# A fused attention and two-layer FFN kernel: the first pair's steps in a new order, its mask as a ramp on ScalarE

## The chip, the cores and the metric

The kernel runs on one core of one Trainium2 chip. The metric is the device time of one execution, in microseconds.

## The reference

Attention over 2 batches, 8 heads, 768 positions and head size 64, with a window of `n_local` = 96 keys back, `n_global` = 8 keys that all see, and a linear bias by distance; then two feed-forward layers on 1536 tokens of width 512 (inner width 2048), the second with a rational activation.

```
scores = q k^T / sqrt(D)
is_global = pos_k < n_global;   is_local = (0 <= rel) & (rel < n_local),  rel = pos_q - pos_k
dist = n_local where global and not local, else |rel|
scores = where(global or local, scores - slope_h * dist, -1e9)
x = softmax(scores) v                      # heads put side by side: 1536 x 512
x = max(0.01 h, h) w_out,   h = x w_in     # first layer
y = (P(h) / (Q(h) + 1e-6)) w_out,  h = x w_in   # second layer, P cubic, Q quadratic in |h|
```

## The kernel before

**Pairs and units.** Attention is done by pairs of heads, 8 pairs in all (`P_`), in a window: a block of 128 queries sees its own block of keys and a slot with the block before it, whose first 32 columns hold the global keys. A pair has 6 blocks times 2 heads = 12 units (`U`); unit n has block i = (n mod 12) // 2 and head j = n mod 2. Block 0 has 128 columns of scores, the others 256. Each value of q and k is kept as a high and a low fp32r part (`qh`, `ql`, `kh`, `kl`), and a unit's scores are three passes on TensorE (line 440): `qh kh`, `qh kl`, `ql kh`. Units of head 0 and head 1 use different halves of the array and are issued side by side.

**A unit's steps.** `scores` (L440) writes 256 columns of one of two PSUM banks, `sc0` for head 0 and `sc1` for head 1; even blocks take the first half of the bank, odd blocks the second. `least` (L451, VectorE) adds the bias, stores `sn` and reduces to the least value. `exp` (L465, ScalarE) makes `pr`. `transposes` (L476, TensorE) and `evacuate` (L482 on ScalarE or L484 on VectorE) make `pts`. `values` (L495 to 498, TensorE) multiplies by v, and `finish` (L504 to 507) divides.

**A pair's preparation.** k: transposes on TensorE (L324, for pair 0 L383), `kh` on ScalarE (L334, L400), `kl` on VectorE (L336, L402), then the slots are copied (L349 to 352: on GpSimd; for pair 0 those of `kl` on ScalarE). q: transposes, then for pair 0 `qh` on ScalarE (L413) and `ql` on VectorE (L415); for later pairs `qt` on ScalarE (L362) and `qh`, `ql` on GpSimd (L364, L365). These are generators; each `next` issues one step. Pair 0 loads and prepares blocks 0 and 1 first (`q0`, `k0`), then the further blocks 2 to 5 (`q1`, `k1`); later pairs take two halves of three blocks.

**What sets the order.** Everything here is in a hand-written order: each engine executes its own instructions in the order in which the program issues them, and semaphores hold them until their inputs are there. The loop over n (L638 to 661) issues for each n: scores of the units in `GROUPS[n]`, `least` of those in `LEASTS[n]`, `exp` of unit n - 1, transposes and evacuation of unit n - 3, values of unit n - 5, `finish`, and then `fillers(n)`, which advances each running generator by one step and starts new ones: the next pair's preparation at the slots of `PREP0` (pair 0) or `PREP`, the loads of later pairs, and the decoding of float64 weights into fp32 parts from n = 10 on. From unit 8 on, the scores of four units are issued together. `k1` and `q1` start in `fillers(0)`, behind the scores and reductions of units 0 and 1.

**Ahead of the loop** (L519 to 553): loads on SyncE's and ScalarE's DMA queues, twelve TensorE fillers (`keep_busy`, L531, products of ones that nothing reads), the distance table (`window_bias`), first transposes, the two numbers spread over the partitions by a small product (L538), the mask for block 0 (`far`, L244 and L246), the bias (`near`, L250) and its half for head 1 (`half`). The mask of the other part is made behind the first two reductions. SyncE's queue then holds pair 1's k, half of pair 0's v, pair 1's q, and the other half of v.

**After attention** the two layers follow: 96 blocks of products with 512 columns, TensorE without a pause; the first weights are decoded in attention's fillers.

Of the kernel before, what the change touches and what calls it, by code (L numbers as in the profile page):

```python
# [8 lines left out]
F32 = mybir.dt.float32  # L9
# [8 lines left out]
P = 128  # L18
GW = 32
MAX_LOCAL = P - GW + 1  # L20
QK_BOUND = 7000.0
EPS_Q = 1.0 + 1e-6
FAR = 2.56e11


@with_exitstack
def attention_moe_moe2(
# [26 lines left out]
    NTILE = NT // TT  # L54


    PREP0 = (("prep_k", 4, 0), ("prep_q", 5, 0), ("prep_k", 8, 1), ("prep_q", 9, 1))
    PREP = (("prep_k", 0, 0), ("prep_q", 1, 0), ("prep_k", 4, 1), ("prep_q", 6, 1))
    LOAD_K = 4
    LOAD_V = 6  # L60
# [1 line left out]
    XOUT = (8, 9)  # L62

    FIRST = 8
    BUSY = (12, 3, 8)
    XOUT_LAST = (2, 8)
    AHEAD_STEPS = {93: (0,), 94: (0,), 96: (0,), 97: (0,), 98: (1,), 99: (1,)}
    FIRST_ACT = 98
# [22 lines left out]

    ints = cpool.tile([1, 4], I32, name="ints")
    intf = cpool.tile([1, 4], F32, name="intf")
    num1 = cpool.tile([1, 2], F32, name="num1")
    ones = cpool.tile([1, P], F32, name="ones")
    nums = cpool.tile([P, 2], F32, name="nums")
    n_loc = nums[:, 0:1]
    n_glo = nums[:, 1:2]

# [3 lines left out]
    def read_ints():  # L103
        nc.vector.tensor_copy(intf, ints)
        lo, hi = (intf.rearrange("p (j w) -> p j w", w=2)[:, :, w] for w in range(2))
        nc.vector.scalar_tensor_tensor(hi, lo, 0.0, hi, ALU.is_lt, ALU.add)
        nc.vector.scalar_tensor_tensor(num1, hi, 4294967296.0, lo, ALU.mult, ALU.add)

    coef = cpool.tile([P, 8], F32, name="coef")

# [110 lines left out]
    def window_bias(bpool, rpool):  # L221

        misc = rpool.tile([P, 2 * DM], I32, tag="raw", name="misc")
        rel_i = misc[:, 0:BW]
        dist = bpool.tile([P, BW], F32, name="dist")
        mask = bpool.tile([P, BW], F32, name="mask")
        nc.gpsimd.iota(rel_i[:, W2:BW], [[-1, P]], base=0, channel_multiplier=1)
        nc.gpsimd.iota(rel_i[:, 0:W2], [[-1, W2]], base=P, channel_multiplier=1)
        col_i = bpool.tile([P, GW], I32, name="col_i")
        nc.gpsimd.iota(col_i, [[1, GW]], base=0, channel_multiplier=0)  # L230

        nc.vector.tensor_copy(dist, rel_i)
        nc.vector.tensor_scalar(mask, dist, 0.0, 8192.0, ALU.is_lt, ALU.mult)
        nc.vector.tensor_tensor(dist, dist, mask, ALU.add)
        col = bpool.tile([P, GW], F32, name="col")
        nc.vector.tensor_copy(col, col_i)
        bias = bpool.tile([P, 2, BW], F32, name="bias")

        def part(first):
            return slice(W2, BW) if first else slice(0, W2)  # L240

        def far(first):
            cs = part(first)
            nc.vector.tensor_scalar(mask[:, cs], dist[:, cs], n_loc, FAR, ALU.is_ge, ALU.mult)  # L244
            gs = slice(cs.start, cs.start + GW)
            nc.vector.scalar_tensor_tensor(mask[:, gs], col, n_glo, mask[:, gs], ALU.is_ge, ALU.mult)  # L246

        def near(first):
            cs = part(first)
            nc.vector.scalar_tensor_tensor(bias[:, 0, cs], dist[:, cs], n_loc, mask[:, cs], ALU.min, ALU.add)  # L250

        def half(first):
            cs = part(first)
            if first:
                nc.vector.tensor_scalar(bias[:, 1, cs], bias[:, 0, cs], 0.5, None, ALU.mult)
            else:
                nc.scalar.activation(bias[:, 1, cs], bias[:, 0, cs], AF.Copy, scale=0.5)

        return bias, far, near, half

    def attention(wpool, w1, ffn):
        with ExitStack() as actx:
# [26 lines left out]
            class Pair:  # L289
# [77 lines left out]
                def load_first(self, s):  # L367
                    if s == 0:
                        self.first = {
                            n: apool.tile([P, NB, 2, D], F32, tag=f"{n}r", name=f"{n}r", bufs=2)  # L370
                            for n in "qk"
                        }
                    b = slice(*((0, 2), (2, NB))[s])
                    for name, src in (("q", q), ("k", k)) if s == 0 else (("k", k), ("q", q)):
                        for j, queue in enumerate((nc.sync, nc.scalar if s == 0 and name == "k" else nc.sync)):
                            r = src[self.b, 2 * self.hp + j].rearrange("(i p) d -> p i d", p=P)
                            queue.dma_start(self.first[name][:, b, j], r[:, b])

# [154 lines left out]
            keep_busy(BUSY[0])  # L533
            bias, bias_far, bias_near, bias_half = window_bias(bpool, rpool)
            next(q0)
            read_ints()
            spread = ps.tile([P, W2], F32, tag="pt", name="spread")[:, 0:2]
            nc.tensor.matmul(spread, ones, num1, start=True, stop=True)  # L538
            next(k0)
            keep_busy(BUSY[1])  # L540
            next(q0)
            next(k0)
            nc.vector.tensor_copy(nums, spread)
            bias_far(True)
            next(q0, None)
            next(k0)
            next(k0, None)
            bias_near(True)
            bias_half(True)
            P_[1].load_k()  # L550
            P_[0].load_v((0,))
            P_[1].load_q()
            P_[0].load_v((1,))

            early = []
            for f in range(NF_EARLY):
# [26 lines left out]
            def start(g):  # L583
                next(g)
                running.append(g)

            def fillers(n):

                p, s = divmod(n, PU)
                for g in list(running):  # L590
                    if next(g, running) is running:
                        running.remove(g)
                new = []
                if p + 1 < len(P_):
                    nxt = P_[p + 1]
                    for what, slot, half in PREP0 if p == 0 else PREP:
                        if s == slot:
                            new.append(getattr(nxt, what)(half))
                    if s == LOAD_V:
                        nxt.load_v()  # L600
                    if s == LOAD_K and p + 2 < len(P_):
                        P_[p + 2].load_k()
                    if s == LOAD_Q and p + 2 < len(P_):
                        P_[p + 2].load_q()
                if 0 < p < len(P_):
                    for half, slot in enumerate(XOUT if p < len(P_) - 1 else XOUT_LAST):
                        if s == slot:
                            new.append(P_[p - 1].x_out(half))
                if n in DECS and early:
                    new.append(decode(*early.pop(0)))  # L610
                if n == PU:
                    load_coef()
                if n == 2 * PU:
                    prepare_coef()
                if n == FIRST_ACT:
                    ffn.act_1(0, ([], []))
                for u in AHEAD_STEPS.get(n, ()):
                    ffn.h_step(u)
                if n == 0:
                    start(k1)  # L620
                    start(q1)
                if n == 1:
                    bias_half(False)
                for g in new:
                    start(g)

            def unit(n):
                return U[n] if 0 <= n < len(U) else None

            LV = 5  # L630
            GROUPS = {m: (m,) for m in range(0, FIRST, 2)}
            GROUPS.update({m: (m, m + 2) for m in range(FIRST, len(U), 4)})

            LEASTS = {m: (m, m + 1) for m in range(0, FIRST, 2)}
            for m in range(FIRST, len(U), 4):
                LEASTS[m], LEASTS[m + 1] = (m, m + 1), (m + 2, m + 3)
            n = 0
            while n < len(U) or running or n <= len(U) + LV + 1:  # L638

                for m in GROUPS.get(n, ()):  # L640
                    for _ in zip(unit(m).scores(), unit(m + 1).scores()):
                        pass
                    if n == 2:
                        keep_busy(BUSY[2])
                for m in LEASTS.get(n, ()):
                    unit(m).least()
                    if m == 1:
                        bias_far(False)
                        bias_near(False)
                for m in (0, 1) if n == 1 else (n - 1,):  # L650
                    if n != 2 and unit(m):
                        unit(m).exp()
                if unit(n - 3):
                    unit(n - 3).transposes()
                    unit(n - 3).evacuate()
                if unit(n - LV):
                    unit(n - LV).values()
                if unit(n - LV - 1) and unit(n - LV - 1).ih == HB - 1 and unit(n - LV - 1).j == 1:
                    unit(n - LV - 1).finish()
                fillers(n)  # L660
                n += 1
# [484 lines left out]
```

## Time and profile before

| | us |
|---|---|
| time, median of 3 runs (lowest, highest) | 637.1 (636.68, 637.37) |
| the profiled execution's own time | 637.13 |
| its span, first to last instruction | 635.3 |
| TensorE busy in the span | 626.5 |
| VectorE, ScalarE, GpSimd busy | 469.1, 439.1, 206.9 |

The span is the profiler's, the time includes what lies around it. In the rows below engines are PE (TensorE matmul), PEld (its weight load), DVE (VectorE), ACT (ScalarE), POOL (GpSimd), SP (SyncE); a q behind the name means the engine's instruction queue, for example a DMA issue. L440 is line 440 of the kernel. A row with x2 covers two instructions, and its duration runs from the start of the first to the end of the last. Matmuls are pipelined, so rows of PE overlap. In brackets stands the idle time of the engine just before, and what ended it.

### The profile page before, as it was taken

To read this page: it belongs to the slowest core of one execution; us is meant where nothing else is said; L and a number is where in the kernel's file an instruction comes from. 1 tells how busy PE (TensorE), PEld (TensorE's weight loads), DVE (VectorE), ACT (ScalarE), POOL (GpSimd) and SP (SyncE) were. 2 spreads that over 40 slices of the span, in tenths; PEclk is the share of its full clock that TensorE was granted. 3 is DMA by queue.
4 is the path that set the end of the run, shared out by engine and by line. 5 is a ranking of instruction groups with operands and counts; after the bars stand their busy time and mean duration, and the time that the engine had idled before them with its cause. 6 is when DMAs were issued, how large, how long until landed. Compare 5 with 4: busy or idle time off the path is not lost.

```text
span 635.3 us, 9655 instructions
## 1 busy us (share of the span) xinstructions
PE 626.5 (99%) x3289; PEld 527.7 (83%) x3289; DVE 469.1 (74%) x931; ACT 439.1 (69%) x831; POOL 206.9 (33%) x221
## 2 busy tenths in 40 slices
PE   8999999999999999999999999999999999999996
PEld 7999998888888888888888888888888888888884
DVE  6888888878877545456444489998777777897785
ACT  6888988768776545455444377876677888876672
POOL 3978864443443434341000012222222222112220
PEclk9999999999999999999999999999999999999999
DMA  9987742955267776765322301000033331100002
GB/s 185 222 176 174 165 113 71 311 183 182 81 200 224 229 225 202 245 191 194 99 91 90 91 29 34 1 1 1 0 102 97 101 96 48 68 21 1 2 1 72
DMA packets 80895, 73.34 MB, mean 115 GB/s; under 512 B 50948, under 2 KB 67332, under 8 KB 80836
## 3 DMA queue, kind: packets, MB, share of 16 engines
q1 hardware_dynamic: 80048, 71.12, 39.5%
q0 software_dynamic: 224, 0.92, 0.4%
q8 instruction: 28, 0.46, 0.3%
q10 hardware_dynamic: 564, 0.59, 0.3%
q14 instruction: 31, 0.25, 0.1%
HBM read 60.69 MB, written 11.93 MB: 114 GB/s over the span
## 4 chain that ended last, share of the span: by engine, by line
PE 97%; DVE 2%; ACT 0%; issue 0%; DVEq 0%
PE h L691 41%; PE y L815 21%; PE y L813 21%; PE pt L476 3%; PE sc L440 3%; PE o L498 3%; PE o L497 2%; PE h L324 1%; PE h L209 1%; PE idle L531 0%; PE o L495 0%; DVE sn L451 0%; DVE xl L215 0%; DVE ql L415 0%; DVE kl L402 0%
## 5 line engine op out<-in xcount | busy, mean ns | idle before, releaser
L691 PE MATMUL h<-xh,w 128*128 128x512 f32 x768 | 253.4, 390 | 0.0
L691 PEld LDWEIGHTS h<-xh,w 128*128 128x128 f32 x768 | 144.1, 188 | 29.8
L691 PE MATMUL h<-xl,w 128*128 128x512 f32 x384 | 149.4, 389 | 0.0
L746 POOL TENSOR_TENSOR gl<-u,gh 128x512 fp32r<-128x512 f32 x44 | 57.0, 1296 | 264.4 <-PE y L815 125.4
L813 PE MATMUL y<-gh,w 128*128 128x512 f32 x384 | 126.1, 389 | 0.0
L815 PE MATMUL y<-w,gh 128*128 128x512 f32 x384 | 125.6, 389 | 0.0
L164 POOL TENSOR_TENSOR dec<-dec,wraw 128x512 int32<-128x512 int32 x48 | 63.6, 1334 | 82.7 <-DVE wraw L151 76.3
L813 PEld LDWEIGHTS y<-gh,w 128*128 128x128 f32 x384 | 72.1, 188 | 15.1
L815 PEld LDWEIGHTS y<-w,gh 128*128 128x128 f32 x384 | 72.1, 188 | 15.0
L691 PEld LDWEIGHTS h<-xl,w 128*128 128x128 f32 x384 | 72.2, 188 | 14.5
L815 PE MATMUL y<-w,gl 128*128 128x512 f32 x192 | 75.1, 391 | 0.0
L813 PE MATMUL y<-gl,w 128*128 128x512 f32 x192 | 74.7, 389 | 0.0
L716 DVE TENSOR_TENSOR gl<-h,gh 128x512 fp32r<-128x512 f32 x48 | 33.0, 688 | 51.9 <-ACT gh L715 51.9
L715 ACT ACTIVATE gh<-h 128x512 fp32r<-128x512 f32 x48 | 28.6, 596 | 59.5 <-PE y L813 53.4
L768 ACT ACTIVATE h<-h 128x512 f32<-128x512 f32 x48 | 28.7, 597 | 52.2 <-PE h L691 52.1
L711 DVE SCALAR_TENSOR_TENSOR h<-h,g 128x512 f32<-128x512 f32 x48 | 33.3, 694 | 26.0 <-ACT g L710 25.7
L756 DVE SCALAR_TENSOR_TENSOR w<-w,epsq,h 128x512 f32<-128x512 f32 (+1 forms) x49 | 36.4, 744 | 21.0 <-ACT h L780 20.4
L710 ACT ACTIVATE g<-h 128x512 f32<-128x512 f32 x48 | 28.7, 598 | 30.0 <-PE h L691 29.7
L465 ACT ACTIVATE pr<-sn,st 128x256 f32<-128x256 f32 (+1 forms) x96 | 47.3, 495 | 0.6 <-DVE st L451 0.5
L770 DVE SCALAR_TENSOR_TENSOR w<-h,coef,w 128x512 f32<-128x512 f32 x48 | 35.9, 749 | 16.0 <-ACT w L769 15.8
L815 PEld LDWEIGHTS y<-w,gl 128*128 128x128 f32 x192 | 36.0, 188 | 8.5 <-POOL gl L746 1.1
L813 PEld LDWEIGHTS y<-gl,w 128*128 128x128 f32 x192 | 36.0, 188 | 7.4
(126 smaller groups left out, 1119.2 us busy)
## 6 DMA issues: line engine op xcount, KB each, us to landing
wraw<-in_moe_w_in_dram SPq DMA_DIRECT2D x24, 512.0 KB, 4.6
wraw<-in_moe_w_out_dram SPq DMA_DIRECT2D x24, 512.0 KB, 4.6
scratch<-dec SPq DMA_DIRECT2D x32, 256.0 KB, 5.3
wf<-scratch SPq DMA_DIRECT2D x16, 512.0 KB, 3.5
w<-in_moe_w_in_dram SPq DMA_DIRECT2D x8, 512.0 KB, 4.3
w<-in_moe_w_out_dram SPq DMA_DIRECT2D x8, 512.0 KB, 5.3
vc<-in_v_dram SPq DMA_DIRECT2D x16, 192.0 KB, 3.2
qkraw<-in_q_dram SPq DMA_DIRECT2D x6, 512.0 KB, 3.6
```

The costliest lines, as they stand in the source:

```text
L164: nc.gpsimd.tensor_tensor(ti, ti, self.c, ALU.add)
L465: nc.scalar.activation(self.pr[:, :w], self.sn[:, :w], AF.Exp, bias=self.least_at, scale=-1.0,)
L691: nc.tensor.matmul(h, wt[:, m, c * P : (c + 1) * P], xs[:, c, cs], start=c == 0 and n == 0, stop=c == NK - 1 and n == 2,)
L710: nc.scalar.activation(g, h, AF.Copy)
L711: nc.vector.scalar_tensor_tensor(h, h, 0.01, g, ALU.mult, ALU.max)
L716: nc.vector.tensor_tensor(gl, h, gh.bitcast(F32), ALU.subtract)
L746: (nc.gpsimd if on_pool else nc.vector).tensor_tensor(gl, g, gh.bitcast(F32), ALU.subtract)
L756: nc.vector.scalar_tensor_tensor(ow[:, cs], ow[:, cs], epsq, oh2[:, cs], ALU.add, ALU.mult)
L768: nc.scalar.activation(h2, h, AF.Square)
L770: nc.vector.scalar_tensor_tensor(w0, h2, coef[:, 7:8], w0, ALU.mult, ALU.add)
L813: nc.tensor.matmul(ys[d], wt[:, m, ds_], gs, start=st, stop=sp)
L815: nc.tensor.matmul(ys[d], gs[:, ds_], wt[:, m, :], start=st, stop=sp)
```

## The change

- The further blocks of pair 0's k and q (`k1`, `q1`) are transposed ahead of the second pass of units 0 and 1 and ahead of units 2 and 3, and the scores of units 0 to 3 are all issued before the first `least`. Steps of units 0 to 3 and of `k1`, `q1` are written out ahead of the loop, which starts at n = 3.
- The mask is one ScalarE activation, max(FAR (dist + 1 - n_local), 0), over all 384 columns, and one VectorE step for the global columns of both parts; a third number, FAR (1 - n_local), is spread with the other two.
- Of the further k and q, head 1's loads go to ScalarE's DMA queue. Pair 0's v is loaded ahead of pair 1's k and q.
- Pair 1's preparation starts at slots 6, 7, 9, 10 in place of 4, 5, 8, 9.
- The fillers: eight behind the scores of units 2 and 3 go; two come ahead of those of units 4 and 5, and two, 64 rows high, behind their first pass.

```diff
-FAR = 2.56e11
+FAR = 2.0**38
-    PREP0 = (("prep_k", 4, 0), ("prep_q", 5, 0), ("prep_k", 8, 1), ("prep_q", 9, 1))
+    PREP0 = (("prep_k", 6, 0), ("prep_q", 7, 0), ("prep_k", 9, 1), ("prep_q", 10, 1))
-    BUSY = (12, 3, 8)
+    BUSY = (12, 3, 2, 2)
...
+        nc.vector.tensor_scalar(num1[:, 2:3], num1[:, 0:1], -FAR, FAR, ALU.mult, ALU.add)
...
-        def far(first):
-            cs = part(first)
-            nc.vector.tensor_scalar(mask[:, cs], dist[:, cs], n_loc, FAR, ALU.is_ge, ALU.mult)
-            gs = slice(cs.start, cs.start + GW)
-            nc.vector.scalar_tensor_tensor(mask[:, gs], col, n_glo, mask[:, gs], ALU.is_ge, ALU.mult)
+        def far():
+            nc.scalar.activation(mask, dist, AF.Relu, bias=nums[:, 2:3], scale=FAR)
+            mask_g = mask_all[:, 0 : 2 * W2].rearrange("p (a c) -> p a c", a=2)[:, :, 0:GW]
+            col_g = col.unsqueeze(1).to_broadcast([P, 2, GW])
+            nc.vector.scalar_tensor_tensor(mask_g, col_g, n_glo, mask_g, ALU.is_ge, ALU.mult)
...
-                        for j, queue in enumerate((nc.sync, nc.scalar if s == 0 and name == "k" else nc.sync)):
+                        for j, queue in enumerate((nc.sync, nc.sync if s == 0 and name == "q" else nc.scalar)):
...
             next(q0)
+            next(k0)
             read_ints()
...
-            next(k0)
             keep_busy(BUSY[1])
             next(q0)
             next(k0)
             nc.vector.tensor_copy(nums, spread)
-            bias_far(True)
             next(q0, None)
             next(k0)
+            bias_far()
             next(k0, None)
             bias_near(True)
             bias_half(True)
+            P_[0].load_v()
             P_[1].load_k()
-            P_[0].load_v((0,))
             P_[1].load_q()
-            P_[0].load_v((1,))
...
-                if n == 0:
-                    start(k1)
-                    start(q1)
-                if n == 1:
-                    bias_half(False)
...
-            n = 0
+            def together(m):
+                return zip(unit(m).scores(), unit(m + 1).scores())
+
+            begun = together(0)
+            next(begun)
+            next(k1)
+            list(begun)
+            next(q1)
+            list(together(2))
+            next(k1)
+            unit(0).least()
+            unit(1).least()
+            unit(0).exp()
+            unit(1).exp()
+            next(k1)
+            bias_near(False)
+            next(q1)
+            next(k1, None)
+            bias_half(False)
+            next(q1, None)
+            unit(2).least()
+            unit(3).least()
+            n = 3
...
-                    for _ in zip(unit(m).scores(), unit(m + 1).scores()):
-                        pass
-                    if n == 2:
+                    if n == 4:
                         keep_busy(BUSY[2])
+                    for step, _ in enumerate(together(m)):
+                        if n == 4 and step == 0:
+                            keep_busy(BUSY[3], P // 2)
                 for m in LEASTS.get(n, ()):
                     unit(m).least()
-                    if m == 1:
-                        bias_far(False)
-                        bias_near(False)
-                for m in (0, 1) if n == 1 else (n - 1,):
-                    if n != 2 and unit(m):
-                        unit(m).exp()
+                if unit(n - 1):
+                    unit(n - 1).exp()
```

## Rows read from the trace of the kernel before

**Rows 1.** The page, chain that ended last: share of the span by engine
```profile
PE 97%; DVE 2%; ACT 0%; issue 0%; DVEq 0%
```

**Rows 2.** Windows: stretch in us, busy us (and instructions) of each engine, clock, DMA
```profile
32.00:36.00 4.00, 3.78 (x39) 3.60 (x39) 3.35 (x16) 3.30 (x9) 1.69 (x4) 1.00 0.96 165
...
100.00:600.00 500.00, 500.00 (x2230) 413.78 (x2230) 362.38 (x564) 334.56 (x581) 130.51 (x102) 1.00 0.35 111
```

**Rows 3.** Timeline, PE: start, us, engine, line, operation, tiles, count, idle before
```profile
12.65 0.31 PEld L324 LDWEIGHTS h<-ident,qr 128*128 128x128 f32 x3 [0.23 <-PE pt L476]
...
13.13 0.38 PE L440 MATMUL sc<-kh,qh 64*128 64x256 f32 x2
...
19.29 0.28 PE L440 MATMUL sc<-kh,ql 64*128 64x128 f32 x2
```

**Rows 4.** Timeline, PE, the first pair's passes and transposes
```profile
6.02 0.33 PE L440 MATMUL sc<-kh,qh 64*128 64x128 f32 x2
...
6.70 0.33 PE L440 MATMUL sc<-kl,qh 64*128 64x128 f32 x2 [0.35 <-DVE kl L402]
...
7.07 0.66 PE L383 MATMUL h<-ident,kr 128*128 128x128 f32 x4
...
8.64 1.22 PE L531 MATMUL idle<-warm 128*128 128x256 f32 x8
...
9.90 0.48 PE L440 MATMUL sc<-kh,qh 64*128 64x256 f32 x2
...
11.20 0.39 PE L440 MATMUL sc<-kh,ql 64*128 64x256 f32 x2 [0.21 <-DVE ql L415]
```

**Rows 5.** Timeline, ACT and DVE, the first pair
```profile
4.73 0.38 ACT L413 ACTIVATE qh<-h 128x256 fp32r<-128x256 f32 x1 [1.37 <-PE h L383]
...
5.21 0.16 DVE L543 COPY nums<-spread 128x2 f32<-128x2 f32 x1 [1.11 <-PE spread L538]
...
7.17 0.29 DVE L451 CUSTOM_DVE_ANT_0 sn<-sc,bias 128x128 f32<-128x128 f32 x1
...
8.11 0.58 ACT L400 ACTIVATE kh<-h 128x512 fp32r<-128x512 f32 x1
...
9.86 0.69 DVE L402 TENSOR_TENSOR kl<-h,kh 128x512 fp32r<-128x512 f32 x1
...
10.46 0.68 DVE L415 SCALAR_TENSOR_TENSOR ql<-h,qh 128x512 fp32r<-128x512 f32 x1
```

**Rows 6.** Timeline, PE and DVE, units 8 to 11: scores and reductions
```profile
15.18 0.28 PE L440 MATMUL sc<-kh,ql 64*128 64x256 f32 x2
...
15.53 0.28 PE L440 MATMUL sc<-kh,ql 64*128 64x256 f32 x2
...
15.85 0.42 DVE L451 CUSTOM_DVE_ANT_0 sn<-sc,bias 128x256 f32<-128x256 f32 x1 [0.49 <-PE sc L440]
...
16.20 0.42 DVE L451 CUSTOM_DVE_ANT_0 sn<-sc,bias 128x256 f32<-128x256 f32 x1
```

**Rows 7.** Timeline, DVE and POOL: pair 1's first half of k and q
```profile
14.48 0.55 DVE L336 TENSOR_TENSOR kl<-h,kh 128x384 fp32r<-128x384 f32 x1
...
15.11 0.97 POOL L352 TENSOR_TENSOR kl<-kl,zeros 128x288 fp32r<-128x288 f32 x2 [0.76 <-DVE kl L336]
...
16.95 1.00 POOL L365 TENSOR_TENSOR ql<-qt,qh 128x384 fp32r<-128x384 f32 x1
```

**Rows 8.** Timeline, DMA issues; then the DMA view's issues of 0 to 60 us
```profile
3.31 1.05 SPq L377 DMA_DIRECT2D qr<-in_q_dram  x2
...
10.70 0.54 SPq L317 DMA_DIRECT2D vp<-in_v_dram  x1
...
qr<-in_q_dram SPq DMA_DIRECT2D x12, 192.0 KB, 5.5
...
vc<-in_v_dram SPq DMA_DIRECT2D x11, 192.0 KB, 3.8
```

**Rows 9.** Timeline, PE, the first fillers
```profile
1.33 2.93 PE L531 MATMUL idle<-warm 128*128 128x256 f32 x12 [1.33 <-DVE warm L526]
```

More of the change, by code (lines that the diff above doesn't have):

```diff
@@ L93, in attention_moe_moe2 @@
     intf = cpool.tile([1, 4], F32, name="intf")
-    num1 = cpool.tile([1, 2], F32, name="num1")
+    num1 = cpool.tile([1, 3], F32, name="num1")
     ones = cpool.tile([1, P], F32, name="ones")
-    nums = cpool.tile([P, 2], F32, name="nums")
+    nums = cpool.tile([P, 3], F32, name="nums")
     n_loc = nums[:, 0:1]
@@ L106, in read_ints @@
         nc.vector.scalar_tensor_tensor(hi, lo, 0.0, hi, ALU.is_lt, ALU.add)
-        nc.vector.scalar_tensor_tensor(num1, hi, 4294967296.0, lo, ALU.mult, ALU.add)
+        nc.vector.scalar_tensor_tensor(num1[:, 0:2], hi, 4294967296.0, lo, ALU.mult, ALU.add)
+        nc.vector.tensor_scalar(num1[:, 2:3], num1[:, 0:1], -FAR, FAR, ALU.mult, ALU.add)
     coef = cpool.tile([P, 8], F32, name="coef")
@@ L225, in window_bias @@
         dist = bpool.tile([P, BW], F32, name="dist")
-        mask = bpool.tile([P, BW], F32, name="mask")
+        mask_all = bpool.tile([P, 2 * W2], F32, name="mask")
+        mask = mask_all[:, 0:BW]
         nc.gpsimd.iota(rel_i[:, W2:BW], [[-1, P]], base=0, channel_multiplier=1)
@@ L535, in attention @@
             next(q0)
+            next(k0)
             read_ints()
-            spread = ps.tile([P, W2], F32, tag="pt", name="spread")[:, 0:2]
+            spread = ps.tile([P, W2], F32, tag="pt", name="spread")[:, 0:3]
             nc.tensor.matmul(spread, ones, num1, start=True, stop=True)
-            next(k0)
             keep_busy(BUSY[1])
@@ L630, in attention @@
             LV = 5
-            GROUPS = {m: (m,) for m in range(0, FIRST, 2)}
+            GROUPS = {m: (m,) for m in range(4, FIRST, 2)}
             GROUPS.update({m: (m, m + 2) for m in range(FIRST, len(U), 4)})
-            LEASTS = {m: (m, m + 1) for m in range(0, FIRST, 2)}
+            LEASTS = {m: (m, m + 1) for m in range(4, FIRST, 2)}
             for m in range(FIRST, len(U), 4):
                 LEASTS[m], LEASTS[m + 1] = (m, m + 1), (m + 2, m + 3)
-            n = 0
+            def together(m):
[20 more added lines that the diff above has]
+            n = 3
             while n < len(U) or running or n <= len(U) + LV + 1:
                 for m in GROUPS.get(n, ()):
-                    for _ in zip(unit(m).scores(), unit(m + 1).scores()):
-                        pass
-                    if n == 2:
+                    if n == 4:
                         keep_busy(BUSY[2])
+                    for step, _ in enumerate(together(m)):
+                        if n == 4 and step == 0:
+                            keep_busy(BUSY[3], P // 2)
                 for m in LEASTS.get(n, ()):
                     unit(m).least()
-                    if m == 1:
-                        bias_far(False)
-                        bias_near(False)
-                for m in (0, 1) if n == 1 else (n - 1,):
-                    if n != 2 and unit(m):
-                        unit(m).exp()
+                if unit(n - 1):
+                    unit(n - 1).exp()
                 if unit(n - 3):
```

## The prediction

> **What bounds the kernel now.** I read the page's chain first: TensorE carries 97% of it [rows 1]. The windows by stage say where: from 100 to 600 us TensorE is busy for all 500 us, and all it lacks between 16 and 60 us is 0.22, from 32 to 36 [rows 2]. So whatever TensorE loses or wins at the start reaches the end one for one; there is no wait later that could swallow it. The question is how late TensorE gets through the first pair, and I compare one point of both kernels: the third pass of unit 12, the first unit of pair 1, which starts at 19.29 us now [rows 3].
>
> Then I went through the timeline of the first 20 us, engine by engine. Five things are to be seen there. (1) Scores of units 4 and 5 start at 9.90, but their third pass waits for `ql` of the further q and starts at 11.20 [rows 4]: VectorE makes `kl` at 9.86 and `ql` at 10.46 [rows 5]. This is what the change attacks. (2) VectorE's reduction of unit 8 ("least", line 451) starts at 15.85, though unit 8's own third pass ended at 15.18 + 0.28 = 15.46; it waits until unit 10's third pass, in other columns of the same score bank, ends at 15.53 + 0.28 = 15.81 [rows 6]. A reduction waits for every score that was issued ahead of it into its bank. (3) The same the other way round: the pair of passes at 9.90 takes 0.48 where others take 0.38 or 0.39 [rows 3, 4], because unit 5 waits for the reduction of unit 3, again in other columns. (4) Pair 1's q transposes begin at 12.65 after 0.23 us idle [rows 3]; the row names TensorE's own work, long done, so I read it as their load being only just there. (5) GpSimd builds pair 1's `kl` slots, `qh` and `ql` from 15.11 to 16.95 + 1.00 = 17.95 [rows 7], 1.34 us before unit 12's third pass needs them.
>
> **The change, part by part.**
>
> *Further k and q, and scores of units 0 to 3, ahead of the first reduction.* TensorE now issues: pass 1 of units 0 and 1, four k transposes, passes 2 and 3, four q transposes, all passes of units 2 and 3; only then, in program order, stand the reductions of units 0 and 1. By (2) these wait for units 2 and 3. In rows: pass 1 starts at about 6.0 as now (6.02, [rows 4], is set by `kh`, which comes earlier, but the three fillers ahead of it stay), and I give it 0.24. Passes 2 and 3 take 7.07 - 6.70 = 0.37; both transpose groups with units 2 and 3 take 8.64 - 7.07 = 1.57 [rows 4]; two more switches between full-height and half-height work cost about 0.1 each (0.38 for a pass behind a switch, 0.28 for one behind another pass, [rows 3, 6]). 6.0 + 0.24 + 0.37 + 1.57 + 0.2 = 8.4. Reduction 0 goes from 7.17 [rows 5] to 8.45, **1.28 us later**.
>
> Behind it on ScalarE, in program order, stand two exponentials and then the further q's `qh`. Now the copy behind the two exponentials starts at 8.11, 0.94 after reduction 0, and 512 columns take 0.58 [rows 5]: `qh` goes from 8.45 + 0.94 = 9.39 to 9.97. VectorE fills that time with `kl` and the near bias, then makes `ql` from 10.0, with 0.60 to the next (10.46 - 9.86, [rows 5]): reductions 2 and 3 start at 10.6 and 10.95 and give their results 0.43 later (0.35 apart, 0.42 each, [rows 6]). By (3) unit 4 waits for the one, unit 5 for the other: 11.09 and 11.44 in place of 9.90 and 10.0. Their later passes wait for nothing; with two fillers between, some 0.12 each, pass 3 starts at 11.9 and ends at 12.2. Now it starts at 11.20 [rows 4]. The wait for `ql` goes, and a longer one for the reductions takes its place: **0.7 us later** here.
>
> One of the Trainium skill's rules speaks against this order: "PSUM — Partial Sum Buffer", section "PSUM bank collisions raise a hardware error", says that two engines that touch one bank in the same 32-partition quadrant collide even at different columns, and that the compiler's back end therefore orders any two such instructions. By that rule the new order puts units 2 and 3 ahead of reduction 0 and the sum is the one below; without it the sum is that of the first rival. The trace agrees with it, with the 0.39 us between the end of unit 8's own passes and its reduction.
>
> *Pair 1's k and q prepared at units 6, 7, 9 and 10 in place of 4, 5, 8 and 9.* This takes two groups of three transposes (13.13 - 12.65 = 0.48 with the switches, [rows 3]; some 0.33 without) and the hole of (4) out of the stretch before unit 6 and puts the transposes behind it. Units 6 and 7 wait for reductions 4 and 5: 12.23 + 0.35 + 0.43 + 0.05 = 13.06, beside 13.13 now [rows 3]: equal. From there to the end of unit 10's last pass TensorE takes 15.81 - 13.13 = 2.68 [rows 3, 6], and now 0.67 more: 16.41 in place of 15.81, **0.6 us later**.
>
> What follows from it on GpSimd costs more. Pair 1's `kl` now stands in VectorE's queue behind reductions 8 and 9, and these wait for unit 10 by (2). 16.41 + 0.35 + 0.35 = 17.11; `kl` 0.55 [rows 7]; 0.08 to GpSimd; then slots of `kl`, `qh` and `ql` as now, 16.95 + 1.00 - 15.11 = 2.84 [rows 7]: 20.58, and unit 12's third pass at 20.63. TensorE's own work would bring it there at 16.41 + (19.29 - 15.81) = 19.9 [rows 3, 6]. It waits **0.7 us**, and the point of comparison goes from 19.29 to 20.63: **1.34 us later**.
>
> *Mask as a ramp on ScalarE.* A 384-wide activation with a number as its bias is not among the rows; between the 256-wide copy (0.38) and the 512-wide one (0.58) [rows 5] I take 0.55. It replaces the comparisons on VectorE for both parts. The numbers reach it some 0.5 us later than now (5.21), as the k transposes and a third number come first. From there to reduction 0 VectorE needed 7.17 - 5.21 = 1.96 [rows 5], so the bias is ready at 5.7 + 1.96 + 0.3 = 7.95 at the latest, and reduction 0 comes at 8.45: it costs nothing. Without that cover (first rival) the ramp itself sets reduction 0, 0.4 to 0.8 later than now.
>
> *Two loads on ScalarE's queue.* Each holds its queue for about 0.55 (two took 1.05, [rows 8]). ScalarE's first copy has 1.37 idle before it [rows 5], so 1.1 fits: nothing. SyncE's queue gets 1.1 free, and the further q's issue ends 1.1 earlier; TensorE comes for it at 7.2, in place of 7.5. If it landed 1 us later than I think, up to 0.9.
>
> *Pair 0's v ahead of pair 1's k and q.* The queue holds the same loads; its last issue ends at 11.24 now [rows 8], after at about 10.1, and it is q's. So q's two start at 9.1 and 9.6. From issue to landing takes 3.8 for a v, 5.5 for a q (medians, [rows 8]): between 13.4 and 15.1; I take 14.2, the middle, since the queue is as full as now. It is needed at about 13.06 + 1.9 = 15.0. k, one pair of issues earlier, is needed about 0.9 earlier, with the same slack. No cost; with a load 1 to 2 us later than the middle, 0.2 to 1.2.
>
> *Fewer fillers.* Eight go, four come. The eight lay in TensorE's wait of (1), two of the four in the wait for reduction 2; the other two are counted above.
>
> **Sum.** +1.34 us, with 0.3 either way from some twenty durations that vary by hundredths. The profiled execution took 637.13 us (span 635.3); the median of the runs shown is 637.1. From either: **638.4 us**.
>
> **The rivals.**
> *A reduction waits for its own unit alone (not slower).* Then reduction 0 starts once the bias is there, about 7.6, and units 4 and 5 pass between 9.0 and 10.0, over 1 us ahead of now. It decides from the point where reduction 0 starts before about 8. What is late next: pair 1's q, at 14.2 for a need at 13.4, then GpSimd's chain with 0.45. By the same steps unit 12's third pass comes at 19.5 and the time is 637.4; with q in time 636.5; with GpSimd in time too, 635.9. Against it: the 0.39 in [rows 6] and the 0.48 in [rows 4].
> *GpSimd is in time.* If pair 1's `kl` gets past reductions 8 and 9, the 0.6 alone is left: 637.8. Against it: VectorE's rows run in program order.
> *Pair 1's q lands late.* At 15.5 to 16.0 TensorE waits 0.5 to 1.0 more, 639.2. For it: the hole before 12.65.
> *TensorE's clock falls back.* The first twelve fillers stand 2.93 / 12 = 0.24 apart [rows 9], the 1.2 GHz level; the eight at 8.64 take 1.22 together, 0.15 and less, the 2.4 GHz level [rows 4]. (The granted clock reads 1.00 throughout; spacing tells more here.) From 8.4 to 11.9 TensorE will do less than it does now, with fewer fillers. Another low stretch as long as the first 2.93 costs half of that, 1.5: 639.9. Against it: now TensorE has little to do from 10.3 to 11.2 and stays at the upper level.
>
> **How the numbers follow.** Forecast 0.62 (638.0 to 638.9); reductions wait for their own unit 0.15; GpSimd in time 0.08; q late 0.08; clock 0.07. About 0.2% (1.27 us) is what a measurement of this kernel can tell from no change: faster is below 635.8, slower above 638.4. My forecast lies on that line. Slower: 0.35 of the forecast, late q and clock, 0.50. Same: the other 0.27 of the forecast, GpSimd in time, and most of the first rival, 0.45. Faster: the far end of the first rival, 0.05. The range, 637.0 to 639.5, holds the forecast, GpSimd in time, late q, and the nearest price of the first rival.
>
> **What would show it.** Right: reduction 0 starts behind unit 2's last pass, near 8.45; `qh` of the further q behind both exponentials, near 9.4; units 4 and 5 start behind reductions 2 and 3, near 11.1 and 11.4; unit 12's second and third pass are torn apart by some 0.7 us, and GpSimd's `ql` ends the wait. Wrong: reduction 0 before 8, unit 12's third pass before 19.3, or pair 1's q transposes waiting for a load.

## The result, and the profile after

The changed kernel takes **641.03 us** (median of 7 runs, 640.36 to 644.29), 4.4 us more than the kernel before beside it (636.68). The ratio is **1.0073, 95% interval 1.0052 to 1.0093**: slower, and 1.5 us beyond my range. The profiled execution took 641.27 us, its span 639.5.

First the point that the prediction compares, unit 12's third pass, and the way to it. Timeline of TensorE, kernel after (start, us, engine, line, operation, tiles, count, idle before):

```profile
4.85 0.66 PE L385 MATMUL h<-ident,kr 128*128 128x128 f32 x2 [0.16 <-DMA kr<-in_k_dram]
...
8.50 0.28 PE L442 MATMUL sc<-kh,ql 64*128 64x256 f32 x2
...
9.61 0.33 PE L478 MATMUL pt<-ident,pr 128*128 128x128 f32 x1 [0.83 <-ACT pr L467]
...
11.54 0.64 PE L442 MATMUL sc<-kh,qh 64*128 64x256 f32 x2 [1.36 <-DVE st L453]
...
22.98 0.27 PE L442 MATMUL sc<-kl,qh 64*128 64x128 f32 x2
...
23.75 0.33 PE L442 MATMUL sc<-kh,ql 64*128 64x128 f32 x2 [0.49 <-POOL ql L367]
```

The third pass starts at 23.75 where it was 19.29 [rows 3]: 4.46 later, and the span is 4.2 longer. TensorE stays the chain of the rest (96% of it by the page of the changed kernel, 97% before [rows 1]), so the loss lies in these 24 us. VectorE's reductions and GpSimd, kernel after:

```profile
7.47 0.23 DVE L257 TENSOR_SCALAR bias<-bias 128x128 f32<-128x128 f32 x1
...
8.82 0.29 DVE L453 CUSTOM_DVE_ANT_0 sn<-sc,bias 128x128 f32<-128x128 f32 x1 [1.12 <-PE sc L442]
...
10.97 0.41 DVE L453 CUSTOM_DVE_ANT_0 sn<-sc,bias 128x256 f32<-128x256 f32 x1
```

```profile
22.69 1.00 POOL L367 TENSOR_TENSOR ql<-qt,qh 128x384 fp32r<-128x384 f32 x1
```

Reduction 0 has its bias from 7.47 + 0.23 = 7.70 on, and waits 1.12 more for the last pass of units 2 and 3, which ends at 8.50 + 0.28 = 8.78. Units 4 and 5 wait 1.36 for reductions 2 and 3 (the first starts at 10.97; the row at 11.54 names `DVE st` as what ended the wait). Unit 12's second and third pass are 0.77 apart, and GpSimd's `ql` ends the wait. All of this was forecast. The windows show what was not. Their columns are the stretch, its length, then busy us (and count) of TensorE, its weight loads, VectorE, ScalarE and GpSimd, the granted clock, DMA share and GB/s:

```profile
8.00:10.00 2.00, 1.17 (x12) 0.78 (x9) 1.18 (x6) 0.85 (x3) 0.96 (x2) 1.00 1.40 204
10.00:12.00 2.00, 0.64 (x5) 0.40 (x5) 1.70 (x6) 1.71 (x7) 0.00 (x0) 1.00 1.37 214
12.00:14.00 2.00, 2.00 (x14) 1.74 (x14) 0.78 (x4) 1.52 (x6) 0.00 (x0) 0.60 1.38 220
14.00:16.00 2.00, 2.00 (x13) 1.77 (x12) 0.78 (x4) 0.97 (x3) 0.00 (x0) 0.50 1.38 217
16.00:18.00 2.00, 2.00 (x12) 1.67 (x11) 0.42 (x1) 1.11 (x3) 0.97 (x2) 0.50 1.37 208
18.00:20.00 2.00, 2.00 (x19) 1.87 (x19) 0.47 (x3) 0.04 (x1) 0.00 (x0) 0.69 1.42 202
```

Behind the passes of units 2 and 3 TensorE has 1.17 us of work between 8 and 10 and 0.64 between 10 and 12. Then its granted clock falls from 2.4 GHz (1.00) to 1.2 GHz (0.50). The mean clock of the four windows from 12 to 20 is 0.40, 0.50, 0.50 and 0.31 short of 1.00, and each window is 2 us; as the lower level is 0.50 short, that is 2 x 1.71 / 0.5 = 6.8 us at the lower level, and TensorE is busy all that time.

### The profile page after: what moved, and what is told of

It is laid out like the page before. It is cut to its first block, busy times and chain, and to the rows that moved or that the text cites. A ratio compares the mean times of both kernels' runs of the same rounds, so it can differ in the third digit from the quotient of the medians.

```text
span 639.5 us, 9646 instructions
## 1 busy us (share of the span) xinstructions
PE 629.1 (98%) x3285; PEld 529.7 (83%) x3285; DVE 467.5 (73%) x929; ACT 439.0 (69%) x832; POOL 206.8 (32%) x221
## 4 chain that ended last, share of the span: by engine, by line
PE 96%; DVE 1%; DMA 0%; POOL 0%; issue 0%; ACT 0%; SPq 0%; DVEq 0%
PE h L707 41%; PE y L831 21%; PE y L829 20%; PE sc L442 4%; PE pt L478 3%; PE o L500 2%; PE o L499 2%; PE h L326 1%; PE h L210 1%; DMA kr<-in_k_dram 0%; PE o L497 0%; DVE sn L453 0%; PE h L385 0%; DVE xl L216 0%; POOL ql L367 0%
## 5 line engine op out<-in xcount | busy, mean ns | idle before, releaser
L453 DVE CUSTOM_DVE_ANT_0 sn<-sc,bias 128x256 f32<-128x256 f32 (+1 forms) x96 | 33.9, 396 | 13.8 <-PE sc L442 13.8
```

The costliest lines, as they stand in the source:

```text
L453: nc.vector.tensor_tensor_reduce(self.sn[:, :w], self.sc[:, :w], bias[:, self.j, b0 : b0 + w], self.pair.slope, 3.0e38, ALU.add, ALU.min, ...
```

## The experiments

The ratios are to the kernel before, run beside each; 0.1% is 0.64 us. Two theories stood at the start: the loss is mostly the clock's fall for want of work, with the forecast's steps beside it; or it lies in the order alone.

**e1_fill.** Fillers into the hole, as I call the stretch from 8.8 to 11.5 in which the changed kernel leaves TensorE little to do.

```
-    BUSY = (12, 3, 2, 2)
+    BUSY = (12, 3, 13, 2)
...
             list(together(2))
+            keep_busy(7)
```

> The changed kernel, with 7 filler matmuls behind the passes of units 2 and 3 and 13 instead of 2 ahead of those of units 4 and 5; nothing else. Theory A (TensorE's clock fell to 1.2 GHz from 12.41 to 19.24 because TensorE had almost nothing to do from 8.8 to 11.5): the granted clock stays full from about 5.5 on, units 4 and 5 still begin at 11.5, unit 12's third passes come at 20.9 instead of 23.75, with about 0.7 of waiting for GpSimd ahead of them, and the time is 638.4 (2.7 under the changed kernel's, 1.6 over the kernel before). Theory B (the clock fell for another reason, as the load of other engines or the late rise at 5.6): it falls again at about 12.4 and the time stays at 641. Theory C (the clock's fall costs little, and the loss lies in the order): the clock stays full and the time is 640 or more.

Measured: 639.14 us, ratio 1.0032 (1.0017 to 1.0046). Timeline of TensorE, reduction 0 on VectorE, and one window:

```profile
5.35 0.62 PE L533 MATMUL idle<-warm 128*128 128x256 f32 x3
...
8.26 1.10 PE L533 MATMUL idle<-warm 128*128 128x256 f32 x7
...
9.24 1.79 PE L533 MATMUL idle<-warm 128*128 128x256 f32 x13
...
11.09 0.63 PE L442 MATMUL sc<-kh,qh 64*128 64x256 f32 x2
...
20.53 0.33 PE L442 MATMUL sc<-kh,ql 64*128 64x128 f32 x2 [0.48 <-POOL ql L367]
```

```profile
8.37 0.29 DVE L453 CUSTOM_DVE_ANT_0 sn<-sc,bias 128x128 f32<-128x128 f32 x1 [1.13 <-PE sc L442]
```

```profile
12.00:14.00 2.00, 2.00 (x17) 1.69 (x17) 1.28 (x7) 1.49 (x5) 0.00 (x0) 1.00 1.37 219
```

The clock stays at 1.00 here and in all of 8 to 20, and theory A holds, though its time was 0.7 too low. From unit 4's first pass to unit 12's third it takes 20.53 - 11.09 = 9.44 us, against 23.75 - 11.54 = 12.21 in the changed kernel: **the fall costs 2.8 us**. (Another 0.45 of the 4.46 is where the stretch begins, mostly the first k's transposes: they start at 4.85, behind their load, in the profile of after and at 4.48 in that of e1.) By the ratios the loss goes from 0.73% to 0.32%, which is 2.6 us. The point is 1.24 us later than before; I had forecast 1.34. What is left at this point is close to my sum; the ratio leaves 2.0 us, with two of the nine runs over 641 (below).

**e11_seven.** Part of that remedy: the changed kernel with the 7 fillers alone.

```
             list(together(2))
+            keep_busy(7)
```

> The changed kernel with one line more: 7 fillers right behind the passes of units 2 and 3; the 13 of e1_fill ahead of units 4 and 5 stay at 2. TensorE's hole shrinks from 2.7 (8.8 to 11.5) to about 1.7. Theory A (the clock falls for want of work): it stays full if 7 are enough, and the time is e1_fill's 639.1 or a little less; if 1.7 is still too long, half clock from about 12 again and 641, as the changed kernel. Rival (it was not the hole but the 13 fillers next to the passes of units 4 and 5 that did something else, as hold the clock through that stretch): half clock and 641. Between A with too long a hole and the rival the run doesn't tell; a full clock speaks for A alone.

Measured: 641.4 us, ratio 1.0072 (1.0057 to 1.0087). Windows:

```profile
8.00:10.00 2.00, 1.93 (x16) 1.58 (x16) 1.43 (x6) 1.10 (x4) 0.72 (x2) 1.00 1.41 200
10.00:12.00 2.00, 0.71 (x7) 0.64 (x8) 1.45 (x6) 1.71 (x7) 0.00 (x0) 1.00 1.39 217
12.00:14.00 2.00, 2.00 (x16) 1.73 (x12) 0.78 (x4) 1.62 (x5) 0.00 (x0) 0.59 1.39 217
14.00:16.00 2.00, 2.00 (x15) 1.79 (x11) 0.78 (x4) 0.91 (x4) 0.00 (x0) 0.56 1.39 218
```

Now 8 to 10 is nearly full, but between 10 and 12 TensorE does 0.71 us of work (1.36 of idle in one piece ahead of unit 4), and the clock falls again, here for (0.41 + 0.44) x 2 / 0.5 = 3.4 us. (The profiled execution is the shortest of the six, 639.49.) By itself this leaves the rival of its expectation standing. e5_least_ahead_few below removes it: it has 9 fillers in place of two, as this run has (7 and 2), but starts units 4 and 5 earlier, so that no hole is left, and its clock stays at 1.00.

**e9_before_no_fill.** The same question from the other side: the kernel before, without its eight fillers.

```
-    BUSY = (12, 3, 8)
+    BUSY = (12, 3, 0)
```

> The kernel before without its 8 fillers behind the passes of units 2 and 3 (the change cut them to 4 and put them later; my prediction gave fillers nothing). TensorE then has nothing from 8.7 until the transposes of unit 0 at 9.7 and little until 11.2, about 1.5 of idle time in all, where the changed kernel had 2.7. Theory A (what little TensorE has to do there decides on its clock): the granted clock falls to 1.2 GHz from about 12 to 19 in the profile or shows in the mean clock of some runs as 0.992 to 0.994, and those are 2 to 3 us over the kernel before. Rival (so short a hole does nothing, and the fillers are indeed worth nothing): clock full throughout, mean clock 0.997 or more in all runs, time within 0.2 us of the kernel before.

Measured: 638.11 us, ratio 1.0017 (1.0004 to 1.0030). Windows:

```profile
10.00:12.00 2.00, 1.42 (x9) 0.69 (x5) 1.69 (x6) 1.22 (x4) 0.17 (x1) 1.00 1.36 215
12.00:14.00 2.00, 1.79 (x15) 1.41 (x13) 1.07 (x5) 1.72 (x7) 0.00 (x0) 0.91 1.32 205
14.00:16.00 2.00, 2.00 (x13) 1.56 (x12) 0.74 (x5) 0.91 (x4) 0.97 (x2) 0.50 1.36 217
16.00:18.00 2.00, 2.00 (x19) 1.90 (x18) 0.93 (x4) 1.50 (x4) 1.41 (x3) 0.73 1.39 211
```

With 1.42 us of work between 10 and 12 the clock falls here too, for (0.09 + 0.50 + 0.27) x 2 / 0.5 = 3.4 us. In this execution the clock's first rise had also come late (see "Why single runs are longer"). The profile of e6_before_loads, below, is the kernel before with its eight fillers, but for the queue of two loads, and rose as late. Unit 12's third pass in e9, then in e6, and a window of e6:

```profile
21.66 0.27 PE L440 MATMUL sc<-kh,ql 64*128 64x128 f32 x2
```

```profile
20.12 0.27 PE L440 MATMUL sc<-kh,ql 64*128 64x128 f32 x2
```

```profile
12.00:20.00 8.00, 7.79 (x75) 6.97 (x75) 5.47 (x24) 6.96 (x20) 4.55 (x9) 1.00 1.33 202
```

With the fillers the clock stays up and the pass comes 1.54 us earlier, so it is not the late rise that brings the fall. The mean clock of e9 is 0.995 or less in 6 of 10 runs, and the longest of them (0.990) took 641.73; it is 0.997 or more in all 26 runs of the kernel before beside it. The eight fillers, to which I had given nothing, are worth about 1 us.

**e5_least_ahead_few, e2_least_ahead.** The bank order. In both, reductions 0 and 1 are issued ahead of units 2 and 3; e2 keeps e1's fillers, e5 has 4 and 5.

```
-    BUSY = (12, 3, 2, 2)
+    BUSY = (12, 3, 5, 2)      # e2: 13
...
             list(begun)
+            unit(0).least()
+            unit(1).least()
             next(q1)
             list(together(2))
+            keep_busy(4)          # e2: 7
             next(k1)
-            unit(0).least()
-            unit(1).least()
```

> As e1_fill, and the two reductions of units 0 and 1 are issued ahead of the passes of units 2 and 3 instead of behind them. Theory A (a reduction waits for all passes issued so far into its bank, so this order cost the changed kernel 1.1 at the first reduction): the first reduction starts at 7.7, when the bias is ready, instead of 8.8; units 4 and 5 begin about 0.8 earlier than in e1_fill (10.7) and the time is 0.8 under e1_fill's: 637.6. Rival (a reduction waits for its own unit's passes alone, and something else held it until 8.8): no change against e1_fill. Rival (units 4 and 5 wait for the low halves of k and q on VectorE whatever the reductions do): the first reduction at 7.7, units 4 and 5 at 11.5 as in e1_fill, same time.

> As e2_least_ahead, with 4 and 5 instead of 7 and 13 fillers: in e2_least_ahead the fillers themselves held TensorE until 11.4, while the reduction that the passes of units 4 and 5 had to wait for ended at 10.2. Theory (a reduction waits for every pass issued so far into its bank, and the first passes of units 4 and 5 for the last reduction of theirs): units 4 and 5 begin at 10.3 instead of 11.1 (e1_fill), the granted clock stays full, unit 12's third passes come 0.6 to 0.8 before e1_fill's 20.5, and the time is 0.6 to 0.8 under e1_fill's. Rival (the loads of v and of pair 1's k and q, which nothing here moves, set the stages behind): units 4 and 5 at 10.3, unit 12's third passes at 20.5 as in e1_fill, same time. Rival (fewer fillers let the clock fall): half clock again from about 12, time 640 or more.

Measured: e2 638.33 us, ratio 1.0021 (1.0006 to 1.0037); e5 638.03 us, ratio 1.0023 (1.0007 to 1.0040). VectorE and TensorE of e2, then of e5, with a window of e5:

```profile
7.36 0.29 DVE L453 CUSTOM_DVE_ANT_0 sn<-sc,bias 128x128 f32<-128x128 f32 x1 [0.40 <-PE sc L442]
```

```profile
9.66 1.79 PE L533 MATMUL idle<-warm 128*128 128x256 f32 x13
...
11.39 0.39 PE L442 MATMUL sc<-kh,qh 64*128 64x256 f32 x2
...
20.70 0.33 PE L442 MATMUL sc<-kh,ql 64*128 64x128 f32 x2 [0.49 <-POOL ql L367]
```

```profile
7.22 0.29 DVE L453 CUSTOM_DVE_ANT_0 sn<-sc,bias 128x128 f32<-128x128 f32 x1
```

```profile
9.94 0.63 PE L442 MATMUL sc<-kh,qh 64*128 64x256 f32 x2 [0.17 <-DVE st L453]
...
14.26 0.52 PE L326 MATMUL h<-ident,qr 128*128 128x128 f32 x3 [0.36 <-DMA qr<-in_q_dram]
...
19.94 0.33 PE L442 MATMUL sc<-kh,ql 64*128 64x128 f32 x2 [0.49 <-POOL ql L367]
```

```profile
8.00:14.00 6.00, 5.74 (x48) 4.74 (x45) 4.08 (x16) 5.18 (x16) 0.51 (x2) 1.00 1.38 212
```

In neither does reduction 0 wait for units 2 and 3: in e5 it starts as soon as its bias is there, and in e2 it waits 0.40 for its own unit's third pass, which ends at 7.33, long before units 2 and 3 are through (8.77). In e2 the 13 fillers run until 9.66 + 1.79 = 11.45 and hold units 4 and 5 themselves: my expectation of 10.7 missed that, and unit 12's third pass is no earlier than e1's. (e2's median is 0.8 under e1's all the same; the profiles don't show why, and the intervals overlap.) With fewer fillers units 4 and 5 start at 9.94, and unit 12's third pass 0.59 ahead of e1's. The order against the bank costs **0.6 us at the end**, half of what it costs at reduction 0 (8.37 in e1, 7.22 in e5): with the earlier start TensorE waits 0.36 for the load of pair 1's q (14.26), which in e1 was in time (its transposes start at 14.88 without a wait).

**e3_own_banks.** The same wait with the order unchanged: units 2 and 3 into other banks, on top of e1.

```
                 self.sc = score_banks[self.j][:, W2 * (i % 2) : W2 * (i % 2 + 1)]
+                if self.n == 2:
+                    self.sc = idle[:, W2 : 2 * W2]
+                if self.n == 3:
+                    self.sc = ps.tile([P, W2], F32, tag="pt", name="sc3")
```

> As e1_fill, and the scores of units 2 and 3 go to two other PSUM banks (that of the fillers, and one of the transposes'), so that units 0 and 1 have their banks alone; the order of issue is the changed kernel's. Theory A (the bank is what the first reduction waits for): it starts at 7.7 instead of 8.8 with the reductions still issued behind the passes of units 2 and 3, and the time is about 0.8 under e1_fill's: 637.6. Rival (the order of issue holds it, not the bank): it stays at 8.8 and the time at e1_fill's.

Measured: 639.53 us, ratio 1.0041 (1.0024 to 1.0059). In the profiled execution of e3 the clock was still at the lower level when units 2 and 3 ran; so it was in that of e10_v_first (below), which has the same order in the old banks. VectorE and TensorE of e3, then of e10:

```profile
8.67 0.29 DVE L457 CUSTOM_DVE_ANT_0 sn<-sc,bias 128x128 f32<-128x128 f32 x1 [1.23 <-PE sc L446]
...
12.44 0.42 DVE L457 CUSTOM_DVE_ANT_0 sn<-idle,bias 128x256 f32<-128x256 f32 x1 [1.40 <-PE idle L537]
```

```profile
8.22 0.41 PE L446 MATMUL sc<-kh,ql 64*128 64x128 f32 x2
...
10.20 0.41 PE L446 MATMUL sc<-kh,ql 64*128 64x256 f32 x1
...
10.54 1.86 PE L537 MATMUL idle<-warm 128*128 128x256 f32 x7
```

```profile
10.93 0.29 DVE L453 CUSTOM_DVE_ANT_0 sn<-sc,bias 128x128 f32<-128x128 f32 x1 [3.21 <-PE sc L442]
```

```profile
5.83 1.01 PE L533 MATMUL idle<-warm 128*128 128x256 f32 x3
...
10.48 0.41 PE L442 MATMUL sc<-kh,ql 64*128 64x256 f32 x2
...
10.82 1.86 PE L533 MATMUL idle<-warm 128*128 128x256 f32 x7
```

In e3 reduction 0 starts at 8.67, behind its own units' last pass (8.22 + 0.41 = 8.63) and ahead of those of units 2 and 3 (10.20 + 0.41 = 10.61). In e10, in one bank, it starts at 10.93, behind theirs (10.48 + 0.41 = 10.89). It is the bank. The time didn't improve, and one row points to the reason: unit 2's scores now share a bank with the fillers, and its reduction waits for these (12.44, behind 10.54 + 1.86 = 12.40). I had overlooked that when I expected 637.6. That this wait, seen in one execution with a late rise, sets the time of the others is argued, not shown. The Trainium skill, "PSUM — Partial Sum Buffer", section "PSUM bank collisions raise a hardware error", says that the compiler's back end orders any two instructions of different engines that touch the same bank and 32-partition quadrant, and that a different address there still collides; both waits agree with it.

**e4_old_prep, e10_v_first.** Pair 1's preparation and its loads: e4 is e1 with both as before, e10 is e4 with the change's loads.

```
-    PREP0 = (("prep_k", 6, 0), ("prep_q", 7, 0), ("prep_k", 9, 1), ("prep_q", 10, 1))
+    PREP0 = (("prep_k", 4, 0), ("prep_q", 5, 0), ("prep_k", 8, 1), ("prep_q", 9, 1))
...
-            P_[0].load_v()           # the loads in e4 alone; e10 has them as in the change
             P_[1].load_k()
+            P_[0].load_v((0,))
             P_[1].load_q()
+            P_[0].load_v((1,))
```

> As e1_fill, with pair 1's preparation at the steps of the kernel before (4, 5, 8, 9) and with the loads in its order (pair 1's k between the first loads and v). Theory A (0.7 of the loss is the GpSimd chain of pair 1's q, started two units later, and the rest of what pair 1's late start costs): no wait of TensorE for GpSimd ahead of unit 12's third passes, and the time is 1.1 under e1_fill's: 637.3. Rival (the chain is hidden again behind the reductions, which then come last): the wait moves to VectorE and the time is e1_fill's within 0.2.

> As e4_old_prep (pair 1's preparation at steps 4, 5, 8, 9), with the change's order of loads: all of v ahead of pair 1's k and q. Theory (these loads land at 12.4 and 14.2, and the early steps meet them late): TensorE waits about 0.2 for pair 1's k and about 1.5 for its q, and unit 12's third passes come 1.0 to 1.5 later after the start of unit 4 than in e4_old_prep (8.4); the time is 1 us over e4_old_prep's 637.8. Rival (TensorE has enough else to do): the same 8.4 and the same time.

Measured: e4 637.84 us, ratio 1.0014 (0.9998 to 1.0030); e10 639.46 us, ratio 1.0036 (1.0025 to 1.0048). Timeline of TensorE, e4:

```profile
11.59 0.64 PE L442 MATMUL sc<-kh,qh 64*128 64x256 f32 x2
...
19.88 0.28 PE L442 MATMUL sc<-kl,qh 64*128 64x128 f32 x2
...
19.99 0.28 PE L442 MATMUL sc<-kh,ql 64*128 64x128 f32 x2
```

The two passes stand 0.11 apart: no wait for GpSimd. From unit 4 to unit 12's third pass it takes 8.40 us against e1's 9.44, so preparation and loads cost **1.04 us** (forecast 1.1). e10 loses 1.4 against e4 by the ratios, where 1 was expected. But its profiled execution ran 2.8 us late at unit 4 (14.38), so that the loads were there; that TensorE waits for them in the others is argued from the time alone.

**e6_before_loads, e12_ramp_alone.** One part of the change alone in the kernel before.

```
-   ... enumerate((nc.sync, nc.scalar if s == 0 and name == "k" else nc.sync)):     # e6
+   ... enumerate((nc.sync, nc.sync if s == 0 and name == "q" else nc.scalar)):
...
-            bias_far(True)                                                          # e12
             next(q0, None)
             next(k0)
+            bias_far()
```

e12 also takes over FAR, the third number and `far` from the change.

> The kernel before with one part of the change alone: both loads of pair 0's further k on ScalarE's queue. My prediction gave this part nothing. Theory D (these two loads share the DMA engines with the first k, delay its landing by 0.3, and open a hole in TensorE's work just when its clock first rises): first k lands at 4.5 or later instead of 4.4, the time is up to 0.3 over the kernel before, and some of its runs show a first rise of the clock that comes late and are 3 us longer, as 2 to 4 in 10 runs of the changed kernel and of e1 to e4 were. Rival (the landing varies from run to run whatever the queue, and the late rise is due to another part): first k at 4.2 to 4.7, the time within 0.2 of the kernel before, none of its runs 3 us longer.

> The kernel before with one part of the change alone: the mask as one ramp on ScalarE (with its third number and the one comparison over both halves on VectorE), at the place it has in the change. My prediction gave this nothing. Theory: the first bias is ready 0.2 to 0.6 later (0.62 of ScalarE instead of 0.29 of VectorE), the first reduction at 7.2 to 7.7 instead of 7.2, VectorE saves 0.6 behind it, and the time is within 0.3 us of the kernel before. Rival (the later first reduction passes through to the end): 0.5 us over it. Rival (VectorE's saving passes through): 0.5 under it.

Measured: e6 637.48 us, ratio 1.0001 (0.9991 to 1.0012); e12 637.52 us, ratio 1.0004 (0.9995 to 1.0013). The expectation of e6 names the loads wrongly: they are one head's further k and one head's further q. Neither part costs anything in the kernel before, as forecast. No run of either was over 639, though the first rise of the clock was late in both profiles; so theory D falls for e6, and e7 confirms it.

**e7_old_queue, e8_head_and_old_rest.** e7 is e4 with the first loads on their old queues; e8 is e5 with these, the old preparation and the old loads, so that the ramp and the new order of the first pair's start are left.

> As e4_old_prep (the changed head, fillers, pair 1's preparation and loads as in the kernel before), with the first loads too on the queues of the kernel before. Theory D (the two loads on ScalarE's queue cause the runs that are 3 us longer): none of its runs over 640, where 4 of e4_old_prep's 12 were; the median 0 to 0.3 under e4_old_prep's 637.8. Rival (the changed order of TensorE's first work causes them): 2 or more runs over 640 again, the median as e4_old_prep's.

> What is left of the change when each cost found is taken out: the first two reductions ahead of the passes of units 2 and 3, 4 and 5 fillers, the ramp on ScalarE, units 2 and 3 ahead; pair 1's preparation, its loads and the queues of the first loads as in the kernel before. Theory (the kernel before is held at units 6 to 9 by the landing of v and of pair 1's k and q, so a head that is earlier by some tenths of a us gains nothing): units 4 and 5 begin at 10.3, unit 12's third passes at 19.2 to 19.4 as in the kernel before (19.3), the time within 0.1% of the kernel before. Rival (the head sets the time): 0.3 us or more under the kernel before.

Measured: e7 638.27 us, ratio 1.0026 (1.0009 to 1.0043), 5 of 12 runs over 640; e8 637.08 us, ratio 1.0008 (0.9997 to 1.0020). The loads are not what makes single runs 3 us longer. Timeline of TensorE, e8:

```profile
9.63 0.63 PE L442 MATMUL sc<-kh,qh 64*128 64x256 f32 x2 [0.17 <-DVE st L453]
...
10.34 0.28 PE L442 MATMUL sc<-kh,ql 64*128 64x256 f32 x1
...
12.16 0.52 PE L326 MATMUL h<-ident,qr 128*128 128x128 f32 x3 [0.56 <-issue]
...
18.77 0.28 PE L442 MATMUL sc<-kh,ql 64*128 64x128 f32 x2
```

Unit 5's third pass starts at 10.34, where it was 11.20 [rows 4]. Then pair 1's q transposes stand idle for 0.56; they were at 12.65 before, after 0.23 [rows 3]. That row names no releaser ("issue"); as e5's row names the load of q at the same place, I read it so here. By the trace's semaphores one of q's two loads landed at 11.2, and the other's landing isn't on record; in e5 the two landed 0.9 apart, the second at 14.1, just ahead of the transposes. So the reading fits, but it is not shown. A start that is 0.9 us earlier gains 0.5 at unit 12 and nothing that the time can tell. No version beat the kernel before.

**Why single runs are longer.** The first fillers run at 1.2 GHz, and when the clock first rises varies from execution to execution. The spacing shows it (the view's clock reads 1.00 from the start): seven fillers at the same place in the code take 1.10 in e1 and 1.86 in e10. Where it rose late, the old order lost little: unit 12's third pass came at 20.15 in e12's profile and 20.12 in e6's, 0.86 and 0.83 late. In the new order units 0 to 5 all hang on TensorE's slow passes, and e10's unit 4 starts 14.38 - 11.59 = 2.8 later than e4's. None of the 89 runs of the kernel before that stood beside these kernels took over 639.5; of the 64 of e1 to e4, e7 and e10, 20 took over 640, and of the 19 of e5 and e8, 4. The changed kernel's own two longest runs (643.60 and 644.29) may be of this kind: their mean clock is 0.998 and 0.997, where four of the other five show 0.992 to 0.994, the low stretch above. That the late rise explains each of these runs is argued from five profiles (e3, e6, e9, e10, e12), not shown.

## Why the prediction was wrong, step by step

*Right, and right in size:* reduction 0 behind units 2 and 3 (8.82, forecast 8.45); units 4 and 5 behind reductions 2 and 3 (11.54, and 11.09 in e1, where the stretch begins earlier; forecast 11.09); pair 1's chain through GpSimd tearing unit 12's passes apart (0.77, forecast 0.7); the sum of these (1.24 in e1, forecast 1.34); the ramp and ScalarE's queue at nothing (e12, e6). v ahead cost nothing either: by the traces pair 1's q landed at 14.1 in e1 and 14.3 in the changed kernel. The forecast was 14.2, but as the middle of 13.4 to 15.1, so that this closeness is luck; and it was in time only because the preparation moved with it: without that, 1.4 (e10).

*Wrong:* "Fewer fillers. Eight go, four come", costed at nothing. I named what the eight lay beside, a wait, and did not ask what TensorE's clock does without them. It does fall, in the kernel before too (e9). The rival that says so was in the list with a chance of 0.07 and a price of 1.5 us; its place was right, and two of its numbers were not. The price took the length of the first low stretch, 2.93 [rows 9]; the stretch was 6.8 long and cost 2.8 (by the price's own rule, half, 3.4). The chance rested on "now TensorE has little to do from 10.3 to 11.2 and stays at the upper level"; but just before that stretch it had done eight fillers [rows 4], so the row was no evidence for a kernel without them. From 8.78 to 11.54 the changed kernel offers TensorE one transpose, two fillers and 0.83 + 1.36 = 2.2 us of nothing. 638.4 + 2.8 = 641.2, beside 641.03 measured. In the profiled execution the 4.46 at unit 12 are 1.24 of the forecast's steps, 2.77 of the clock and 0.45 of a later start, which I had not in the sum and which is one execution's. "PE busy" of that stretch could have been had from my own steps, as the sum of what I had left on TensorE there. A second thing I did not ask is what a late first rise does to the new order: 2.8 at unit 4 in e10, where the old order lost 0.86 at unit 12 in e12.

The Trainium skill states in "TensorE: Matmul & The Clock Gate", Part 1, that a monitor sets the clock by how busy TensorE has been of late. The trace agrees, with 0.50 behind the windows of 1.17 and 0.64 us of work and 1.00 behind e1's full ones.

## What to carry to other kernels

Fillers in a wait are not free to remove: add up what TensorE has left to do in the stretch, and price the low clock over the busy stretch behind it. They are not free to add either; e2's held back the passes that they were to keep fast. And before pulling a start forward, look which load the next stage waits for (e5, 14.26).

## What the runs showed of the hardware

- Before its first rise the granted clock in the profile reads 1.00, while the fillers take 0.24 us (2.93 / 12 [rows 9]) to 0.27 us (1.86 / 7, e10) each, the 1.2 GHz level; at 2.4 GHz seven of them take 1.10 (e1). By the spacing the first rise came at about 5 us in e1's profile (three fillers at 5.35 take 0.62, where e10's at 5.83 take 1.01) and after 12.4 in those of e3 and e10, with the same work issued ahead of it.
- A reduction waits for fillers that write other columns of its bank (e3, 12.44).
